# Changing idle products, a first load and the place of one state product in a decayed-attention and gated feed-forward kernel

## The chip, the core and the metric

The kernel runs on one core of a Trainium2 chip. The metric is the device time of one launch in microseconds; the kernel before takes 227.4 us. Every timed run also gives its span, from the first to the last profiled instruction, which is mostly 1.7 to 2.0 us less. Runs of the kernel before agree within 0.3 us.

The engines are called PE (matrix products), DVE and ACT (element-wise work), POOL (GpSimd, which here also issues most loads) and SP. Times such as "18.32" are microseconds from the start of the span.

## The reference, cut to what matters

```python
# attention with a decay per head, in blocks; q, k, v: (4, 8, 768, 64) float32
for b in range(nb):
    intra = einsum(qb, kb) * Dmask;  intra = einsum(intra, vb)
    inter = einsum(qb * lam_pow, kv_state)
    out[:, :, sl] = intra + inter
    kv_state = lam_block * kv_state + einsum(kb * rev_pow, vb)
# then, with x = out as (3072, 512) and d_ff = 1536:
gate = 1 / (1 + exp(-(x @ w_gate)))
return (gate * (x @ w_val)) @ w_out
```

The kernel walks through six blocks of 128 positions. In each it computes the attention of all 32 batch-heads, then twelve "units" of the feed-forward part: a gate product of four matrix products with 512 columns, a sigmoid on ACT, a value product of the same size, and their elementwise product on DVE. It then projects to the output.

## The kernel before: the parts that matter

In the traces PE runs the products in the order in which the program issues them (block 0's state product, whose keys were ready at 20.47 us, starts only after value 4, at 24.96), and that order is by hand. At the start, where operands are still on their way, "idle products" of zeros keep PE streaming, so that its clock is released to full rate early (at 7.00 us in the trace of this kernel, against 18.15 us in the first trace of the changed one, whose idle products are shorter).

```python
zero = const.tile([128, 2 * C], FP32, tag="zero")        # C = 128
...
load(0, "k", 0, 2)          # block 0: k of batches 0 and 1, issued by POOL, float32 -> bf16
load(0, "k", 2, 4)
load(0, "q", 2, 3)          # q of batches 0 and 1 come by the ACT and SP queues, as float32
load(0, "q", 3, 4)
...                         # v, then the first pieces of w_gate (WG) and w_val (WV)

def idle(n):
    for i in range(n):
        nc.tensor.matmul(wm[:, :2 * C], lhsT=zero[:, :C], rhs=zero, ...)
...
idle(5)
nc.vector.tensor_copy(Q[0][:, 0], q01[0])
piece_tq0([0])              # transposes of q, batch 0
make_mask(0)
idle(1)
piece_tq0([1])
piece_tk0(0)                # transposes of k, batches 0 and 1
make_mask(1)
idle(1)
piece_s(0, [0]) ...         # scores; piece_m masks them on DVE
piece_tq0([2])
idle(1)
...
gv(0, 1)                    # unit 1 of block 0
make_lamq()                 # table of decay powers for later blocks: ten small DVE operations
for ft in (2, 3): ...       # gates of units 2 and 3, then their values
gv(0, 4)                    # gate 4, value 4
c(0, 0, 1)                  # block 0's state product, keys decayed by POOL ("kd") times v
...
gv(0, 5, 6, 7)
```

Gate and value products and one half of the state product share three PSUM buffers ("ff"). A buffer comes free when ACT (gate) or DVE (value, state) has read it: value 4 waits 0.18 us for DVE in the trace below.

## Time and profile before

| | before |
|---|---|
| median of 6 runs, one of them 457.0 (without that slow first run: 227.37) | 227.44 us |
| span of the profiled run | 225.6 us |
| PE busy | 218.8 us, 97% |
| chain of waits | PE 90%, POOL 4%, DMA 3% |

The page's first parts for the kernel before: busy time by engine with the number of instructions, then busy tenths in 40 slices of 5.6 us each.

```profile
PE 218.8 (97%) x1746; PEld 117.5 (52%) x1768; DVE 104.2 (46%) x191; ACT 79.1 (35%) x149; POOL 80.8 (36%) x76
...
PE   7989999999999999999999999999999999999994
...
PEclk9999999999999999999999999999999999999999
DMA  6999999999999991999021999921820012100022
```

PE is full from the fourth slice on, so what can be gained or lost lies in the first 26 us. There the chain of waits runs through POOL's load issues and then a load. The timeline of PE for the kernel before shows it; its columns are start, length of the merged group, engine, line, operation, output and inputs, shape, count, and in brackets the idle time before it with what ended it.

```profile
1.19 4.64 PE L217 MATMUL wm<-zero 128*128 128x256 f32 x10 [1.19 <-DVE ip L124]
5.79 0.61 PE L244 MATMUL tq<-ident,qb 128*128 128x128 bf16 x4
6.19 1.05 PE L217 MATMUL wm<-zero 128*128 128x256 f32 x2
7.08 0.39 PE L244 MATMUL tq<-ident,qb 128*128 128x128 bf16 x4
...
14.75 0.81 PE L437 MATMUL gp<-XT,WG 128*128 128x384 bf16 x4
...
18.32 1.04 PE L429 MATMUL vp<-XT,WV 128*128 128x512 bf16 x4 [0.34 <-DMA WV<-in_moe_w_val_dram]
19.34 1.90 PE L437 MATMUL gp<-XT,WG 128*128 128x512 bf16 x8
...
22.80 1.03 PE L423 MATMUL gp<-XT,WG 128*128 128x512 bf16 x4
24.00 1.02 PE L429 MATMUL vp<-XT,WV 128*128 128x512 bf16 x4 [0.18 <-DVE ht L450]
24.96 0.69 PE L407 MATMUL cp<-vb,kd 128*64 128x64 bf16 x32
25.59 1.04 PE L423 MATMUL gp<-XT,WG 128*128 128x512 bf16 x3
```

Three things are to be read. First, four transposes of 128 columns take 0.61 us at 5.79 and 0.39 us at 7.08: the clock was released in between. (The `PEclk` row reads 9 in the slow stretch too. The trace's clock records begin with the release, at 7.00 us here; before its first record the view just prints full clock, 1.00.) Second, value 1 waits for WV's second piece until 18.32, and gate 2 (19.34) starts just after the third piece of WG has landed, at 19.29. Third, value 4 (24.00) waits for a PSUM buffer that DVE still reads, and the state product comes after it. A count of x3 where four products were issued is a missing record.

### The profile page before, as it was taken

The numbers are of one execution on the slowest core, as the hardware profiler recorded it, in microseconds if no ns is written. First come the engines' busy times: TensorE is split into PE (matmuls) and PEld (weight loads), VectorE is DVE, ScalarE is ACT, GpSimd is POOL, SyncE is SP. The second block draws the span as 40 slices with busy tenths as digits, with TensorE's granted clock in tenths as the row PEclk, the third lists the DMA queues.
The fourth block names the chain that finished last, engine by engine and source line by source line (L and its number), as shares of the span: only waits on it lengthen the run. The fifth ranks groups of instructions, "written<-read, shape, count | busy, mean of one in ns | idle before, by whom it ended". The sixth has DMA issues, their size and how long they took to land.

```text
span 225.6 us, 4279 instructions
## 1 busy us (share of the span) xinstructions
PE 218.8 (97%) x1746; PEld 117.5 (52%) x1768; DVE 104.2 (46%) x191; ACT 79.1 (35%) x149; POOL 80.8 (36%) x76
## 2 busy tenths in 40 slices
PE   7989999999999999999999999999999999999994
PEld 5653455788864455444446444446444445444443
DVE  7866746586530522435642345742334850333300
ACT  5554234435422225333115333225333224433221
POOL 8999967973691007940005950000000000000000
PEclk9999999999999999999999999999999999999999
DMA  6999999999999991999021999921820012100022
GB/s 111 155 172 196 188 177 156 156 191 166 157 188 171 221 175 72 217 150 122 1 96 46 145 146 148 75 94 51 188 46 0 3 46 93 49 0 0 0 94 96
DMA packets 105860, 25.72 MB, mean 114 GB/s; under 512 B 95984, under 2 KB 102896, under 8 KB 105840
## 3 DMA queue, kind: packets, MB, share of 16 engines
q0 software_dynamic: 81232, 13.90, 79.7%
q1 hardware_dynamic: 23568, 11.28, 20.8%
q10 hardware_dynamic: 1040, 0.26, 0.5%
q8 instruction: 14, 0.23, 0.4%
q14 instruction: 6, 0.05, 0.1%
HBM read 28.32 MB, written 6.29 MB: 153 GB/s over the span
## 4 chain that ended last, share of the span: by engine, by line
PE 90%; POOL 4%; DMA 3%; issue 1%; DVE 0%; DVEq 0%; POOLq 0%
PE po L486 27%; PE vp L429 21%; PE gp L423 21%; PE gp L458 5%; PE vp L464 5%; DMA WV<-in_moe_w_val_dram 3%; PE sp L302 2%; PE gp L437 2%; PE op L314 2%; POOL vb L96 2%; PE op L326 1%; PE cp L407 1%; PE po L475 1%; POOL kb L96 1%; POOL qb L96 1%
## 5 line engine op out<-in xcount | busy, mean ns | idle before, releaser
L432 DVE TENSOR_TENSOR ht<-sg,vp 128x512 bf16<-128x512 bf16 x56 | 38.5, 687 | 66.8 <-PE vp L429 62.7
L486 PE MATMUL po<-WO,ht 128*128 128x512 bf16 x266 | 61.3, 379 | 0.5
L423 PE MATMUL gp<-XT,WG 128*128 128x512 bf16 x217 | 57.2, 379 | 0.6
L429 PE MATMUL vp<-XT,WV 128*128 128x512 bf16 x220 | 56.6, 379 | 0.5 <-DMA WV<-in_moe_w_val_dram 0.3
L426 ACT ACTIVATE sg<-gp 128x512 bf16<-128x512 f32 x56 | 33.4, 597 | 62.6 <-PE gp L423 62.6
L486 PEld LDWEIGHTS <-ht 128*128 128x128 bf16 x276 | 26.3, 98 | 31.0
L429 PEld LDWEIGHTS <-WV 128*128 128x128 bf16 x224 | 21.8, 98 | 27.4 <-DMA WV<-in_moe_w_val_dram 0.8
L423 PEld LDWEIGHTS <-WG 128*128 128x128 bf16 x224 | 21.4, 98 | 25.3
L489 ACT COPY ob<-po 128x512 f32<-128x512 f32 x23 | 13.5, 585 | 52.3 <-PE po L486 48.4
L199 DVE TENSOR_TENSOR MT<-sp,mask 128x512 bf16<-128x512 f32 x40 | 25.1, 682 | 10.3 <-PE sp L302 10.3
L388 POOL TENSOR_TENSOR sd<-Sb,dec 128x512 f32<-128x512 bf16 x8 | 8.1, 1035 | 43.8 <-DVE Sb L414 43.8
L458 PE MATMUL gp<-XT,WG 128*128 128x256 bf16 x96 | 14.4, 273 | 0.0
L464 PE MATMUL vp<-XT,WV 128*128 128x256 bf16 x96 | 14.4, 273 | 0.0
L468 DVE TENSOR_TENSOR ht<-sg,vp 128x256 bf16<-128x256 bf16 x24 | 10.0, 420 | 8.6 <-PE vp L464 8.6
L461 ACT ACTIVATE sg<-gp 128x256 bf16<-128x256 f32 x24 | 9.2, 383 | 13.0 <-PE gp L458 11.9
L96 POOL DMA_DIRECT2D vb<-in_v_dram x10 | 12.8, 1282 | 1.4 <-DMA kb<-in_k_dram 1.1
L379 POOL TENSOR_TENSOR kd<-kb,kds 128x1024 bf16<-128x1024 bf16 x6 | 11.3, 1903 | 3.1 <-DMA kb<-in_k_dram 3.1
L414 DVE TENSOR_TENSOR Sb<-cp,sd 128x512 bf16<-128x512 f32 x8 | 5.1, 686 | 15.5 <-PE cp L407 15.5
L341 ACT CAST XT<-op 128x512 bf16<-128x512 f32 x19 | 9.9, 598 | 2.1 <-PE op L314 2.0
L458 PEld LDWEIGHTS <-WG 128*128 128x128 bf16 x96 | 9.2, 98 | 1.7 <-issue 0.2
L464 PEld LDWEIGHTS <-WV 128*128 128x128 bf16 x96 | 9.4, 98 | 1.1
L217 PE MATMUL wm<-zero 128*128 128x256 f32 x20 | 8.4, 556 | 1.2 <-DVE ip L124 1.2
(83 smaller groups left out, 159.4 us busy)
## 6 DMA issues: line engine op xcount, KB each, us to landing
out_dram<-ob SPq DMA_DIRECT2D x21, 256.0 KB, 2.2
kb<-in_k_dram POOLq DMA_DIRECT2D x11, 256.0 KB, 10.2
qb<-in_q_dram POOLq DMA_DIRECT2D x9, 256.0 KB, 9.0
vb<-in_v_dram POOLq DMA_DIRECT2D x4, 512.0 KB, 14.1
WO<-in_moe_w_out_dram POOLq DMA_DIRECT2D x3, 512.0 KB, 8.5
WG<-in_moe_w_gate_dram POOLq DMA_DIRECT2D x5, 256.0 KB, 8.4
WV<-in_moe_w_val_dram POOLq DMA_DIRECT2D x5, 256.0 KB, 9.1
qb<-in_q_dram POOLq DMA_DIRECT2D x4, 128.0 KB, 8.3
```

What stands on the lines that cost most here:

```text
L96: nc.gpsimd.dma_start(out=lst[n][:, b0:b1], in_=src[b0:b1, :, sl, :].rearrange("b h s d -> s (b h) d"))
L199: nc.vector.tensor_tensor(out=out.rearrange("p (e x) c -> p e x c", e=2), in0=x.rearrange("p (e x) c -> p e x c", e=2), in1=mask.rearrange ...
L379: nc.gpsimd.tensor_tensor(out=KD[n][:, e], in0=K[n][:, e], in1=kds[:, e::2].unsqueeze(1).unsqueeze(3).to_broadcast([128, B, HP, D]), op=AL ...
L423: nc.tensor.matmul(gp, lhsT=WG[:, mt, fs], rhs=x[:, mt, :], start=(mt == 0), stop=(mt == NMT - 1))
L426: nc.scalar.activation(sg, gp, AF.Sigmoid)
L429: nc.tensor.matmul(vp, lhsT=WV[:, mt, fs], rhs=x[:, mt, :], start=(mt == 0), stop=(mt == NMT - 1))
L432: nc.vector.tensor_mul(HT[n, ft], sg, vp)
L458: nc.tensor.matmul(gp[:, cs], lhsT=WG[:, mt, fs], rhs=x[:, mt, cs], start=(mt == 0), stop=(mt == NMT - 1))
L464: nc.tensor.matmul(vp[:, cs], lhsT=WV[:, mt, fs], rhs=x[:, mt, cs], start=(mt == 0), stop=(mt == NMT - 1))
L468: nc.vector.tensor_mul(HT[n, ft][:, cs], sg[:, cs], vp[:, cs])
L486: nc.tensor.matmul(po, lhsT=HT[n, ft][:, tt * 128:(tt + 1) * 128], rhs=WO[:, ft, :], start=(ft == 0), stop=(ft == NFT - 1))
L489: nc.scalar.copy(ob, po)
```

## The change

The change does three things in the first 26 us. It replaces the ten float32 idle products, each of which the trace shows as two records, with eight bf16 ones, of one record each, that read every second element of a wider zero tile. It splits the first load of k, so that batch 0 can arrive sooner. It puts block 0's state product between gate 4 and value 4, where value 4 was waiting for its buffer anyway.

```diff
-    zero = const.tile([128, 2 * C], FP32, tag="zero")
+    zero = const.tile([128, TCH], BF16, tag="zero")            # TCH = 512
...
-    load(0, "k", 0, 2)
+    load(0, "k", 0, 1)
+    load(0, "k", 1, 2)
     load(0, "k", 2, 4)
...
+    zero2 = zero.rearrange("p (n t) -> p n t", t=2)[:, :, 0].unsqueeze(1).to_broadcast([128, 2, TCH // 2])
     def idle(n):
         for i in range(n):
-            nc.tensor.matmul(wm[:, :2 * C], lhsT=zero[:, :C], rhs=zero, start=True, stop=True,
+            nc.tensor.matmul(wm.rearrange("p (t n) -> p t n", t=2), lhsT=zero[:, :C], rhs=zero2, start=True, stop=True,
...
     make_mask(1)
-    idle(1)
     piece_s(0, [0])
...
     piece_tq0([2])
-    idle(1)
     piece_tq0([3])
...
-    gv(0, 4)
+    g4 = psum()
+    mm_part(g4, WG, 0, 4, 0, TCH)
+    sigm(0, 4, g4)
     c(0, 0, 1)
+    v4 = psum()
+    mm_part(v4, WV, 0, 4, 0, TCH)
+    prod(0, 4, v4)
```

## The prediction

> **What bounds the kernel now.** From 18.3 us on TensorE does: the windows view has PE busy 34.8 of the 35 us from 25 to 60 and 39.7 of 40 from 150 to 190, and the chain of waits is PE products to the end. Before 18.3 us the chain is not PE: it is GpSimd issuing loads (1.26 to 11.18), then 7.09 us of DMA until WV's second piece lands; the value product of unit 1 starts on it at 18.32.
>
> **The idle products.** Before: ten, each two records 427 ns apart in the first microseconds (timeline, 1.19 to 5.79), so 0.85 us apiece. First transposes take 0.61 us per four, from 7.08 on 0.39, so the release fell near 6.7. After: eight, one bf16 pass of 512 columns. Estimate: 0.43 us slow, 0.21 fast (128x512 bf16 products start 0.216 us apart here). I expect the every-second-element read to run at full rate: [...] About 5 us of PE busy time goes, off the chain. The first five then end near 3.4, and PE is idle until the q cast, 5.7. So the release, [...] should slip from 6.7 to roughly 10. From 7 to 14.7 DVE is full (QS, masks, MT: about 8.3 us of work from 6.51), so PE at half rate there mostly fits into the room the idles leave. Expected cost 0 to 0.4 us before 14.75, absorbed by the 18.3 wait; only if the release slips past 16 does it reach the end.
>
> **k as two loads.** GpSimd takes 0.88 us for a 128x8x64 issue, 1.29 for 128x16x64: later issues start 0.5 us later. But landings trail issues by 6 us throughout and DMA moves a steady 155 GB/s from 6 to 12 us: the queue drains at its own rate, with the first bytes now 0.4 us sooner. WV's second piece: 18.3, plus or minus 0.4.
>
> **The state product.** Before: gate 4 at 22.80, value 4 at 24.00 (0.34 us late: its PSUM buffer waits for unit 2's product on DVE), state 24.96, gate 5 at 25.59. After: state fills that gap from about 23.7 to 24.4; value 4 then inherits the buffer of unit 3, freed at 24.54, so it starts near 24.63 and gate 5 near 25.49. Gain 0.1 us on the chain.
>
> **Sum.** 227.37 - 0.1 - 0.15 (loads, uncertain) = 227.1 us, range 226.3 to 228.0. Chances: faster by over 2% 0.01, within 2% 0.97, slower by over 2% 0.02.
>
> **What would show it.** PE busy down by about 5 us at an unchanged span; transposes still 0.6 us per four past 7 us; first k landing about 1 us sooner; value 1 starting within 0.4 us of 18.32; gate 5 0.1 us sooner relative to value 1; all later stages shifted rigidly.
>
> **What would make it wrong.** A clock released only after 16 us (dense products at half rate, up to +2.5 us); strided reads at half rate (idles as long as before; little change in time); loads paced by issue, moving the 18.3 wait by +0.5; the earlier k traffic delaying q of batch 0 and with it the full DVE stretch.

## The result, and the profile after

The changed kernel takes 228.12 us, the median of six runs from 227.71 to 228.88; the kernel before 227.44 us. The ratio is 1.0038, 95% interval 1.0016 to 1.0059. Ratios here are the mean time of one kernel's runs over that of the other's of the same rounds, so they are not quite the ratio of the medians quoted. Executions over 1.5% slower than the fastest of the same kernel are left out of the means. The change thus costs 0.4%: the same within 2%, but slower than the predicted 227.1 and just outside the range to 228.0.

The spread is as telling as the median. The kernel before had a span of 225.6 us in each of eleven runs of the next set of rounds. The changed kernel's six spans are 225.9, 226.1, 226.2, 226.4, 227.1 and 227.1 us. The profiled run is one of the last two.

The page's first parts for the changed kernel:

```profile
PE 219.3 (97%) x1756; PEld 116.2 (51%) x1756; DVE 103.3 (46%) x191; ACT 79.1 (35%) x149; POOL 81.5 (36%) x77
...
PE   4889999999999999999999999999999999999994
...
PEclk9999999999999999999999999999999999999999
```

PE's busy time did not fall, although about 5 us of idle products are gone: the first slices are emptier, but the remaining products ran longer. The timeline of PE for the changed kernel shows where (value products issued by the helper `mm_part` stand there as `gp<-XT,WV`):

```profile
1.19 2.31 PE L220 MATMUL wm<-zero 128*128 128x512 bf16 x5 [1.19 <-DVE ip L124]
5.74 0.61 PE L247 MATMUL tq<-ident,qb 128*128 128x128 bf16 x4 [2.24 <-DVE qb L504]
...
7.03 0.60 PE L247 MATMUL tq<-ident,qb 128*128 128x128 bf16 x4 [0.25 <-ACT qb L166]
...
12.51 1.03 PE L305 MATMUL sp<-QS,KS 64*128 64x128 bf16 x16 [0.46 <-DVE QS L265]
...
16.33 1.44 PE L440 MATMUL gp<-XT,WG 128*128 128x384 bf16 x4
...
18.24 0.82 PE L440 MATMUL gp<-XT,WV 128*128 128x384 bf16 x4
...
20.21 1.03 PE L432 MATMUL vp<-XT,WV 128*128 128x512 bf16 x4
...
24.53 1.03 PE L440 MATMUL gp<-XT,WG 128*128 128x512 bf16 x4
25.48 0.69 PE L410 MATMUL cp<-vb,kd 128*64 128x64 bf16 x32
26.19 1.02 PE L440 MATMUL gp<-XT,WV 128*128 128x512 bf16 x4
27.05 1.03 PE L426 MATMUL gp<-XT,WG 128*128 128x512 bf16 x4
```

The idle products end after 2.31 us instead of 4.64, and PE then stands still for 2.24 us. Transposes are still slow at 7.03. Even the first gate product, at 16.33, takes 1.44 us for the work that took 0.81 us before, and only at 18.24 do four products of that size take 0.82. The trace's clock records put the release at 18.15 us, 11 us later than before. Value 1 starts at 20.21 instead of 18.32 and does not wait for its load at all. From value 1 to gate 5 it is 27.05 - 20.21 = 6.84 us, against 25.59 - 18.32 = 7.27 us before: 0.43 us come back there, part of it because value 1 no longer runs ahead of the loads behind it (from gate 2 on it is 5.98 us, at 21.07 in this trace, against 6.25). From there on all stages are shifted by about 1.45 us to the end.

So in this run the late clock explains the loss. But even the fastest span of the changed kernel, 225.9 us, is above the 225.6 of before, and the prediction had given the loads and the state product gains. So there were two theories: CLOCK, by which the thin idle products cost the time, and LOADS, by which the split k does.

### The profile page after: what moved, and what is told of

Its sections match the earlier page's. It is cut to its first block, busy times and chain, and to the rows that moved or that the text cites. A ratio compares the mean times of both kernels' runs of the same rounds, so it can differ in the third digit from the quotient of the medians.

```text
span 227.1 us, 4278 instructions
## 1 busy us (share of the span) xinstructions
PE 219.3 (97%) x1756; PEld 116.2 (51%) x1756; DVE 103.3 (46%) x191; ACT 79.1 (35%) x149; POOL 81.5 (36%) x77
## 4 chain that ended last, share of the span: by engine, by line
PE 94%; DMA 2%; DVE 1%; ACT 1%; issue 0%; SPq 0%
PE po L489 27%; PE gp L426 21%; PE vp L432 21%; PE gp L461 5%; PE vp L467 5%; PE gp L440 4%; PE sp L305 3%; PE op L317 3%; DMA q1f<-in_q_dram 2%; PE op L329 1%; PE cp L410 1%; PE po L478 1%; DVE MT L198 1%; PE tk L247 0%; ACT qb L166 0%; PE tq L247 0%
## 5 line engine op out<-in xcount | busy, mean ns | idle before, releaser
L435 DVE TENSOR_TENSOR ht<-sg,vp 128x512 bf16<-128x512 bf16 x55 | 37.8, 687 | 66.2 <-PE vp L432 66.2
L426 PE MATMUL gp<-XT,WG 128*128 128x512 bf16 x220 | 56.5, 379 | 0.0
L429 ACT ACTIVATE sg<-gp 128x512 bf16<-128x512 f32 x55 | 32.8, 597 | 60.3 <-PE gp L426 60.3
L77 POOL DMA_DIRECT2D qb<-in_q_dram x8 | 9.4, 1182 | 0.0
```

The costliest lines, as they stand in the source:

```text
L426: nc.tensor.matmul(gp, lhsT=WG[:, mt, fs], rhs=x[:, mt, :], start=(mt == 0), stop=(mt == NMT - 1))
L429: nc.scalar.activation(sg, gp, AF.Sigmoid)
L435: nc.vector.tensor_mul(HT[n, ft], sg, vp)
```

## The experiments

### One part at a time

Four kernels, five rounds each on one chip. In those rounds the kernel before had a median of 227.40 us in 11 runs.

**Old idle products put back into the changed kernel.**

```diff
-    zero = const.tile([128, TCH], BF16, tag="zero")
+    zero = const.tile([128, 2 * C], FP32, tag="zero")
 ...  # and the float32 product, ten of them, as before
```

> The changed kernel with the ten fp32 idle products put back; the k split and the moved state product stay. Theory CLOCK (the thinner idle products let TensorE's clock release slip from 6.7 us to about 17.7, so the first dense products run at half rate): release back near 7 us, the value product of unit 1 within 0.5 us of 18.3, total 227.1 to 227.5, spread of runs under 0.3 us. Rival LOADS (the split k pushes all later loads back and that costs the time): total stays at 228.0 to 228.3.

Measured: 227.76 us (227.64 to 227.78), spans 225.9 to 226.0. The release came at 6.62 us. The spread is gone, but 0.36 us of the loss stay. Neither theory was right alone.

**New idle products alone.**

```diff
 # the kernel before, with only the zero tile, idle() and the two dropped idle(1) of the change
```

> The kernel before with only the idle products changed (bf16, every second element, eight). CLOCK: 228.0 to 229.2, runs spread over about 1 us or more, transposes at 107 ns beyond 7 us in the trace. LOADS: 227.4, as before.

Measured: 227.78 us, from 227.49 to 229.84, with four spans of 225.7 to 225.8 and two of 226.9 and 227.0. The trace is of the fastest run, with the release at 12.21 us. So the new idle products make the spread: in most runs they cost 0.1 to 0.2 us of span, in two of six 1.3 to 1.4. The median is below the 228.0 I expected, since I had taken the first trace of the change, a late one, for the usual case.

**State product alone moved.**

```diff
-    gv(0, 4)
+    g4 = psum(); mm_part(g4, WG, 0, 4, 0, TCH); sigm(0, 4, g4)
     c(0, 0, 1)
+    v4 = psum(); mm_part(v4, WV, 0, 4, 0, TCH); prod(0, 4, v4)
```

> The kernel before with only the state product moved. Both theories: the distance from value 1 to gate 5 shrinks from 7.27 us to about 7.0 us and the total falls by 0.2 to 0.3 us, to 227.1 to 227.2. If it falls by 0.1 or less the gain is taken back later.

Measured: 227.27 us (227.22 to 227.32), 0.13 us less than before, so less than I expected after seeing the trace and near the predicted 0.1; value 1 to gate 5 shrank to 6.91 us, but value 1 itself came 0.22 us later in this trace (from gate 2, at 19.41, to gate 5 it is 6.04 us against 6.25). The interval of the ratio, 0.9982 to 1.0006, includes 1, though all five runs lie below all 11 of the kernel before (227.36 to 227.51). The timeline of PE for this kernel:

```profile
22.87 1.03 PE L437 MATMUL gp<-XT,WG 128*128 128x512 bf16 x4
23.82 0.70 PE L407 MATMUL cp<-vb,kd 128*64 128x64 bf16 x32
24.59 1.02 PE L437 MATMUL gp<-XT,WV 128*128 128x512 bf16 x3
25.45 1.03 PE L423 MATMUL gp<-XT,WG 128*128 128x512 bf16 x4
```

Value 4 starts at 24.59, within 0.04 us of the predicted 24.63, and gate 5 at 25.45 against the predicted 25.49. The mechanism is the predicted one: DVE frees unit 3's buffer at 24.53. That gate 4 came 0.07 us later than in the kernel before makes the closeness of the times partly luck.

**First k alone split.**

```diff
-    load(0, "k", 0, 2)
+    load(0, "k", 0, 1)
+    load(0, "k", 1, 2)
```

> The kernel before with only the first k as two loads. CLOCK: release near 7 us as before; total 227.4 to 227.8, since later landings come about 0.4 us later, of which the wait at 18.3 takes all or part. LOADS: 228.0 to 228.4.

Measured: 227.87 us (227.79 to 227.94), 0.47 us more than before, with hardly any spread and the release at 4.44 us. The split alone costs more time than CLOCK's account left for it (227.4 to 227.8), and less than LOADS asked for. The three parts together, 0.38 for the idle products, 0.47 for the split and -0.13 for the state product, make 0.72 us by the medians; the whole change showed 0.68, or 0.75 if the 457.0 us run is left out of the median before.

### Why does the split k cost time?

All landings behind it come later, by 0.26 to 0.41 us in the table. These are times from the traces' issue times and times to landing. The last two columns are the next two experiments.

| landing, us | before | first k split | second k split | k: one, then three |
|---|---|---|---|---|
| q of batch 0 (ACT queue) | 4.93 | 5.31 | 4.92 | 5.22 |
| k of batch 0 | 7.30 | 6.88 | 7.28 | 6.79 |
| k of batch 1 | 7.30 | 7.71 | 7.28 | 9.34 |
| q of batch 2 | 9.85 | 10.21 | 9.84 | 10.17 |
| v of batch 0 | 11.53 | 11.94 | 11.56 | 11.83 |
| WV, second piece | 18.27 | 18.53 | 18.06 | 17.31 |
| WG, third piece | 19.29 | 19.68 | 19.22 | 18.71 |
| WV, fourth piece | 23.31 | 23.72 | 23.27 | 23.70 |

k of batch 0 gains 0.42 us, but k of batch 1 loses 0.41. It is needed in the same step (both go through the same transposes). And even q of batch 0, which another queue had begun to load before, comes 0.38 us later.

Two theories: PER-LOAD, by which each further load takes about 0.4 us from all behind it, and HEAD, by which the small load matters only where it stands, at the head, while DMA is not yet full. In the next rounds the kernel before had a median of 227.44 us in 9 runs.

**The second k load split instead of the first.**

```diff
     load(0, "k", 0, 2)
-    load(0, "k", 2, 4)
+    load(0, "k", 2, 3)
+    load(0, "k", 3, 4)
```

> The kernel before with the SECOND k load (batches 2 and 3) as two loads, the first k whole. Same number of loads and bytes as with the split first k. Theory HEAD (the small load at the head meets the two q loads of the other queues while DMA is not yet full, and the lost throughput of 3 to 4 us is never regained): q of batch 0 lands at 4.9 as before, all later landings within 0.1 us of before, total 227.4 to 227.5. Rival PER-LOAD (each further load costs about 0.4 us of queue time to all behind it): q of batch 2 lands at 10.2 to 10.3 instead of 9.85, WV's second piece near 18.5, total 227.8 to 227.9.

**As many loads as before, the small one at the head.**

```diff
-    load(0, "k", 0, 2)
-    load(0, "k", 2, 4)
+    load(0, "k", 0, 1)
+    load(0, "k", 1, 4)
```

> The kernel before with k as one batch, then three: as many loads as before, but the small one at the head. HEAD: q of batch 0 lands near 5.3, later loads 0.3 to 0.45 us later than before (WV's fourth piece near 23.7). PER-LOAD: q at 4.9, later landings as before (23.3). The total says little, since k of batch 1 comes late and holds the first block up.

The landings speak for HEAD in both. With the second k split no landing of the table is later than before by more than 0.03 us; with one and three, nearly all are, although there is no further load. (That kernel's total, 228.86 us in its single run, whose state is unknown, is spoiled by k of batch 1, as expected; on the landings of WV's second and WG's third piece, which vary from run to run, it is even earlier.) The windows view shows what happens at the head: one row for 3 to 4 us, first of the kernel before, then of the kernel with the first k split. The last two numbers are the DMA share and the GB/s moved.

```profile
3.00:4.00 1.00, 1.00 (x4) 0.76 (x3) 0.93 (x4) 0.15 (x2) 1.00 (x2) 1.00 0.87 193
```

```profile
3.00:4.00 1.00, 1.00 (x4) 0.76 (x3) 0.87 (x7) 0.00 (x0) 1.00 (x2) 1.00 0.57 124
```

With the second k split it is 202 GB/s, with one and three 146. From 5 to 6 us the first k split moves 201 GB/s against 169, which makes up about half of what was not moved at 3 to 4. From 6 to 7 us all four move 155 to 156 GB/s with a DMA share of 2.43 to 2.45 (the packets' times are summed, so the share can pass 1), and the kernel before goes on at 154 to 158 until 12 us, so the other half is not made up. Why DMA moves less when the first small load of POOL's queue starts sooner, beside the two q loads of the other queues, no run here shows.

But HEAD failed on the total. With the second k split it was 227.76 us (227.68 to 227.78), 0.32 us over the kernel before, though no landing moved. So there is a second cost, and the timelines find it between unit 1 and gate 5. For the kernel before, POOL's decayed keys and DVE's work after value 1:

```profile
16.70 3.77 POOL L361 TENSOR_TENSOR kd<-kb,kds 128x1024 bf16<-128x1024 bf16 x2
...
20.07 0.61 DVE L181 COPY lp<-lam_bc 64x4 f32<-64x4 f32 x2
20.71 1.85 DVE L185 TENSOR_TENSOR lp<-lp 128x4 f32<-128x4 f32 x7
```

And for the kernel with the second k split, with PE's value 4:

```profile
16.92 3.91 POOL L362 TENSOR_TENSOR kd<-kb,kds 128x1024 bf16<-128x1024 bf16 x2
...
19.86 1.19 DVE L182 COPY lp<-lam_bc 64x4 f32<-64x4 f32 x2
21.08 1.85 DVE L186 TENSOR_TENSOR lp<-lp 128x4 f32<-128x4 f32 x7
...
24.32 1.02 PE L430 MATMUL vp<-XT,WV 128*128 128x512 bf16 x4 [0.56 <-DVE ht L451]
```

One more load to issue makes POOL begin the decayed keys 0.22 us later and end them 0.36 us later, at 20.83 instead of 20.47. The two tiny copies that open DVE's table (four columns each) take 1.19 us instead of 0.61, and the seven table products start 0.25 us after POOL's end in both. In all nine traces where DVE reaches these copies while POOL is still at it, the distance is 0.25 to 0.27 us. And in all 14 kept traces the first of the two copies ends within 0.06 us of the end of the POOL instruction then under way, while the second always takes 0.17 us. In five of the 14 that instruction is not the decayed keys but the issue of a load, so these copies end with an issue too. That they wait for POOL is read from these times; what makes them wait, no run shows. DVE then reaches the products of units 2 and 3 late, which hold two of the three PSUM buffers, and value 4 waits 0.56 us where it waited 0.18.

With the first k split the same happens beside the late landings. POOL's keys and PE in that kernel:

```profile
17.14 3.88 POOL L362 TENSOR_TENSOR kd<-kb,kds 128x1024 bf16<-128x1024 bf16 x2
...
19.72 1.90 PE L438 MATMUL gp<-XT,WG 128*128 128x512 bf16 x8
...
23.19 1.03 PE L424 MATMUL gp<-XT,WG 128*128 128x512 bf16 x4
24.51 1.02 PE L430 MATMUL vp<-XT,WV 128*128 128x512 bf16 x4 [0.30 <-DVE ht L451]
...
26.09 1.04 PE L424 MATMUL gp<-XT,WG 128*128 128x512 bf16 x3
```

The keys end at 21.02 and value 4 starts at 24.51, 0.51 us later than before, which is about the loss of that kernel (0.47). The late landings reach value 4 too, by gate 2, which waits for WG's third piece and is 0.38 us late (a piece whose landing varies anyway: 19.75 with the new idle products alone). But they matter less. An estimate: a value product follows its gate by 0.86 us in the later units, so by the landings alone PE could have begun value 4 at 23.19 + 0.86 = 24.05, only 0.05 us later than before. The rest comes by POOL and DVE. In the changed kernel with the old idle products, too, value 4 starts 4.13 us after the keys' end (25.04 and 20.91), as in the kernel with the state product alone (24.59 and 20.46). So most of the cost of the split k seems to be the second one. No run has the first k split with the table out of the way, so these shares are worked out from traces and not tested.

### Moving the table out of the way

If that account is right, the table should not stand before the products of units 2 and 3 at all.

**State product moved, table built in one piece after unit 4.**

```diff
     gv(0, 1)
-    make_lamq()
...
     prod(0, 4, v4)
+    make_lamq()
```

> The kernel before with the state product moved and, besides, the table of decay powers for later blocks built on DVE after unit 4's product instead of before unit 2's. The wait of value 4 for its PSUM buffer should vanish: gate 5 at 25.1 instead of 25.45 us, total 226.9 to 227.1. If the buffer wait was not what holds value 4, it stays at 227.27.

Measured: 227.53 us (227.50 to 228.09), a miss. Gate 5 came at 25.29 us, earlier than in any kernel so far, but the table then filled DVE from 26.17 to 29.42, so the products of units 5 and 6 waited, and with them value 7:

```profile
29.33 1.27 DVE L432 TENSOR_TENSOR ht<-sg,vp 128x512 bf16<-128x512 bf16 x2
...
30.07 1.02 PE L429 MATMUL vp<-XT,WV 128*128 128x512 bf16 x4 [0.29 <-DVE ht L432]
```

The buffer wait had moved from value 4 to value 7 (the next expectation calls it value 8; the trace has it at value 7).

**The same in four parts, one after each of units 4 to 7.**

```diff
-    gv(0, 5, 6, 7)
+    for ft in (5, 6, 7):
+        gv(0, ft)
+        lamq_part(ft - 4)      # part 0 stands after unit 4's product
```

> The kernel before with the state product moved and the table of decay powers built in four parts on DVE, one after each of the products of units 4 to 7. The build as one piece after unit 4 gave gate 5 at 25.29 but then made value 8 wait (total 227.53). In parts of at most 0.9 us each fits beside a unit's 0.69 us product in 1.73 us. Expected: gate 5 near 25.3 and no later wait, total 227.05 to 227.25. If units 5 to 8 still wait, 227.3 or more.

Measured: 227.10 us (226.88 to 227.22) against 227.45 us (11 runs) of the kernel before in the same rounds, ratio 0.9985, interval 0.9973 to 0.9997. This version beats both kernels. Its profiled run is the slowest of its five (value 1 waited until 18.53 for its load); gate 5 came at 25.45, which is 6.92 us after value 1 instead of 7.27, and no value product up to unit 8 waited for a buffer. From value 1 that is no better than with the state product alone (6.91). The gain of the table shows from gate 2 on, which again waited for its load, until 19.53: 5.92 us to gate 5, against 6.04 with the state product alone and 6.25 before.

```profile
19.53 1.90 PE L439 MATMUL gp<-XT,WG 128*128 128x512 bf16 x8
...
25.45 1.03 PE L425 MATMUL gp<-XT,WG 128*128 128x512 bf16 x4
```

**The same with the second k load split besides.**

```diff
+    load(0, "k", 2, 3); load(0, "k", 3, 4)     # instead of load(0, "k", 2, 4)
```

> The same, with the second k load split besides. Theory POOL-DVE (the split second k cost 0.3 us in its own run although no landing moved, because the decayed keys on GpSimd end 0.36 us later and the first table copies on DVE end only with them, so units 2 and 3 free their PSUM buffers late): with the table out of that place the split costs nothing, total within 0.08 us of the unsplit one. Rival LOAD (the extra load costs time by itself): 0.25 to 0.35 us more than the unsplit one.

Measured: 227.12 us (227.06 to 227.25), 0.02 us from the unsplit one. POOL still ended the decayed keys late, at 20.84, but nothing on DVE waited for them any more. The copies still wait for POOL, now for the issue of a load of v that ends at 27.21, but they have room to:

```profile
25.92 1.29 POOL L96 DMA_DIRECT2D vb<-in_v_dram  x1
26.17 1.22 DVE L184 COPY lp<-lam_bc 64x4 f32<-64x4 f32 x2
```

So the second cost is not the load itself, but what its issue pushes back on POOL and, through POOL, on DVE. One control is missing: no run has the state product moved and the second k split with the table in its old place. With the first k split it exists (the old idles put back), and there the moved state product did not absorb the cost: 227.76 against 227.27 us.

### What releases the clock?

The trace's record of the released clock is 218.453 us long in the kernel before and 208.212 us after: 64 and 61 times 3.413 us, and no longer unit fits both. So, as an estimate from these two lengths, the clock changes at the ends of windows of 3.413 us. How busy a window must be is a second estimate from the traces: count each product as its columns at the spacing seen before the release (107 ns for 128), twice the columns for each float32 record, and take the union over each window, counted back from the release.

| trace | windows not released, share of streaming | window that ended in release | release, us |
|---|---|---|---|
| before | 65% | 92% | 7.00 |
| state product alone | 8% | 95% | 4.89 |
| first k alone | 0% | 90% | 4.44 |
| old idles put back | 54% | 78% | 6.62 |
| new idles alone | 23, 39, 60% | 73% | 12.21 |
| changed kernel | 0, 62, 50, 68, 72% | 79% | 18.15 |
| changed kernel, second trace | 62, 24, 61% | 76% | 13.67 |
| ten idles at the start | 12% | 100% | 5.03 |

All eight released at 73% or more, and no window of 72% or less did. Between 72 and 73 this rough count cannot tell; the rows show a limit near three quarters. The rule was made from the first six rows; the last two are of the tests below. By the same count the two kernels with the table in four parts fit as well: 95% and 100% in the window that ended in release, at 4.79 and 6.15 us, and 5% and 41% before it. In one trace, that with k as one and then three, the clock also fell back, at 11.26 us after a window that by the same count streamed 32%, and was released again at 14.67, 3.41 us later: four transposes took 0.40 us at 9.38 and 0.63 us at 12.07. Theory DUTY, an estimate from these traces alone: the first window with about 73% of streaming or more releases the clock, and the windows lie differently in each run (the releases of the table, divided by 3.413 us, leave from 0.02 us, for 13.67, to 3.21 us, for 6.62). Three kernels tested it.

**Ten bf16 idle products at the start instead of five**, so that they last as long as the float32 ones.

```diff
-    idle(5)
+    idle(10)
```

> The changed kernel with ten instead of five idle products at the start, so that they last 4.3 us as the fp32 ones did; still bf16, every second element. Theory DUTY [...]: release between 4.5 and 8 us, total 227.6 to 227.8 with a spread under 0.3 us, as with the old idle products. Rival TYPE (what matters is that the products are fp32, or that they read contiguously): release later than 10 us in some runs, total 228.1 with a spread of about 1 us.

Measured: 227.72 us (227.66 to 227.80), spans 225.9 to 226.0, release at 5.03 us. The rival TYPE falls: bf16 products that read every second element do the work of the float32 ones, if they last about as long (4.22 us here, 4.64 in the kernel before). The idle products' timeline in this kernel:

```profile
1.19 4.22 PE L220 MATMUL wm<-zero 128*128 128x512 bf16 x10 [1.19 <-DVE ip L124]
6.36 0.40 PE L247 MATMUL tq<-ident,qb 128*128 128x128 bf16 x4 [0.95 <-DVE qb L504]
```

**The two dropped idle products put back, as bf16 ones.**

```diff
     make_mask(1)
+    idle(1)
     piece_s(0, [0])
...
     piece_tq0([2])
+    idle(1)
```

> The changed kernel with the two dropped idle products put back as bf16 ones (ten in all, five at the start). DUTY: each adds 0.43 us of streaming to a slow window, about 12 points of share, so the window around 8 to 11 us rises from 68 to about 80 per cent and the release comes by 8 to 12 us in nearly every run; total 227.7 to 228.0, spread under 0.6 us. If only the first five matter: as the changed kernel, 228.1 with spans from 225.9 to 227.1.

Measured: 227.93 us, from 227.78 to 228.54; four spans of 225.9 to 226.0 and one of 226.7. In its trace the scores at 9.19 still ran partly slow and the transposes at 10.59 fast, so the release fell between. Four runs of five are as DUTY expects; the slow one is not, and the spread of 0.76 us is above the 0.6 I expected. The trace has no clock records, so the windows cannot be counted. This test leans to DUTY but does not decide.

**The changed kernel again**, for another trace.

```diff
 # no edit
```

> The changed kernel once more, unaltered, for another trace of it. DUTY: the release falls [...] anywhere from 8 to 18 us, and the span follows it: 225.9 to 226.1 us for a release before 12, 226.9 to 227.1 for one past 16; median 227.9 to 228.3. If span and release are unrelated in this second trace, the clock is not the cause of the spread.

Measured: 228.30 us, from 227.72 to 229.46, with spans of 226.0 (three times), 227.1, 227.1 and 227.3. This time the traced run was the fastest, and its release came at 13.67 us, in the middle of the scores and before the first dense product:

```profile
12.59 1.04 PE L305 MATMUL sp<-QS,KS 64*128 64x128 bf16 x16 [0.46 <-DVE QS L265]
13.56 0.67 PE L317 MATMUL op<-MT,vb 128*64 128x128 bf16 x16
...
15.66 0.81 PE L440 MATMUL gp<-XT,WG 128*128 128x384 bf16 x4 [0.39 <-ACT XT L357]
...
18.72 1.03 PE L432 MATMUL vp<-XT,WV 128*128 128x512 bf16 x4
```

Its span, 226.0 us, is that of the kernels with an early release and the split k (225.9 to 226.1). So in these two traces a release at 13.67 us is swallowed by the waits of the first 18 us, and one at 18.15 costs 227.1 - 226.0 = 1.1 us. Only two of the twelve runs of the changed kernel have a trace, so that the other long spans (five of twelve were 227.1 or more) are also late releases is likely but not shown run by run.

## Why the prediction was wrong

**What bounds the kernel** was right: PE from 18.3 us on, and a load at 18.3 before that. No experiment moved anything behind 35 us by itself; every difference between two kernels was there by unit 8 and constant afterwards.

**Idle products at full rate** was right. The five take 2.31 us, so 0.43 us each (they start about 0.43 us apart), as estimated: for 512 columns that is four times the 107 ns of a 128-column transpose. "About 5 us of PE busy time goes" was wrong in the first trace (218.8 to 219.3 us), because slow products took it back; in the second, with the earlier release, PE busy was 216.4 us.

**"Should slip from 6.7 to roughly 10 ... absorbed by the 18.3 wait"** is the first step that failed. The mechanism was right, and the release past 16 us was even named as the danger, but the size was off: it came at 13.67 and 18.15 us in the two traces. That the work of 7 to 10 us would be enough for the release was my estimate; no trace had shown it. By the count above, the windows there held 50 to 72% of streaming in the first trace, and the one that ended in release 79%. By theory DUTY the windows lie differently in each run, so the cost differs between runs: with the new idle products alone 0.1 to 0.2 us of span in four runs of six and 1.3 to 1.4 in two, 0.38 us of time in the median.

**"The queue drains at its own rate, with the first bytes now 0.4 us sooner. WV's second piece: 18.3, plus or minus 0.4"** is the second step that failed, with "later issues start 0.5 us later" before it, which I took to be harmless. The queue does drain at its own rate, 155 GB/s from 6 us on, and WV's second piece kept to its range in the split alone (18.53). But the sooner first bytes came with less moved in all: 124 GB/s instead of 193 at 3 to 4 us. The first k landed 0.42 us sooner in the split alone (0.54 in the first trace of the change), not 1 us, and everything behind it 0.26 to 0.41 us later. I booked this term as -0.15 us; it measured +0.47. By the traces most of that took a second route I had not looked at: the later issues push POOL's decayed keys back (their end from 20.47 to 21.02), that holds DVE's table up, and that held value 4's buffer.

**The state product** was right. I said 0.1 us; it measured 0.13, and the starts of value 4 and gate 5 fell within 0.04 us of those predicted.

**The sum**: predicted 227.37 - 0.1 - 0.15; measured, by the parts alone, -0.13 + 0.47 + 0.38 = +0.72 us. That the time would stay within 2% was right.

## What to carry to other kernels

Idle products that keep the clock up were worth their length here, not their number: replacing the first five by five that last half as long (2.31 us instead of 4.64) moved the release from 7 us to as late as 18 us, and because, by the estimate above, the windows lie differently in each run, the harm showed as a spread between runs first and in the median second. Splitting the first load did bring its first half sooner, by 0.42 us, but look at everything behind it (0.26 to 0.41 us later here), at the other queues, and at what the issuing engine was to do next. A DVE operation that ends only when a GpSimd instruction does, as the table's first copy did within 0.06 us, is best put where its neighbours have slack, in pieces that fit into that slack: here this gained 0.35 us where the moved product alone gained 0.13.
